# The first DFT step of a long convolution as 64-row by 64-column products, one channel half to a PSUM bank

## The chip, the cores and the metric

The kernel runs on one core of one Trainium2 chip, in one launch. The metric is the time of one execution on the device in microseconds (us). Engines are named as in the profile: PE is TensorE (PEld its weight loads), DVE is VectorE, ACT is ScalarE, POOL is GpSimd, SP is SyncE, which issues most of the DMAs.

## The reference

One block with two halves, on 2048 tokens and 640 channels, all in fp32: a gated long convolution, then an MLP over the tokens. The change lies in the convolution.

```python
def _A_ref(q, k, v, shift_k, ssm_k, ssm_D):
    # short causal convolution of k, 4 taps
    k_shift = sum of k_pad[:, t:t + S, :] * shift_k[:, ks - 1 - t]
    kv = k_shift * v
    # long causal convolution with ssm_k, per channel, over 2 S points
    y_f = rfft(kv padded to 2 S) * rfft(ssm_k padded to 2 S)
    y = irfft(y_f)[:S]
    y = y + kv * ssm_D
    return q * y

mod = (silu(c) @ w_mod)           # six rows: sa, ca, ga, sb, cb, gb
x = A_q
h = layernorm(x) * (1 + ca) + sa
x = x + ga * _A_ref(h, A_k, A_v, A_shift_k, A_ssm_k, A_ssm_D)
h = layernorm(x) * (1 + cb) + sb
x = x + gb * (W2 gelu(W1 layernorm(h)^T))^T
```

## The kernel before

**Tiling.** The 640 channels are worked in five chunks of 128 (`DC`, loop variable `c`). The 2048 tokens are split as n = 32 n1 + n2, with n1 on the 64 rows of a half of the partitions. The two halves of the 128 partitions hold the two halves of a chunk's channels (64 each), written `h` in the code; the 64 channels of a half are paired as index `i` (32 pairs) and `e` (2).

**The Fourier part of a chunk.** Each chunk has these stages, in this order on PE:

- `step1(0, t)`, t = 0 to 3: first DFT step of kv, over n1. The weights (stationary operand) are a column pick of `X`, 64 columns that stand 32 elements apart; the moving operand is `F1`, a constant matrix that holds cosines and sines. `F1` has 128 rows and, for each of cosine and sine (`ri`), 128 columns; it is block diagonal, since `_constants` fills only `f1[h, :, ri, h]`: the rows of channel half h meet the columns of channel half h, and the other two blocks are zero.
- `step1(1, t)`: the same for the convolution's kernel, with weights from `KSP`, whose 64 columns are contiguous. `perm` writes `KSP` into the tile `P`.
- `f2(g)`, g = 0 to 7: the second DFT step, over n2, with weights `W2` and the tile `z` as the moving operand; ACT copies the kernel's half into `kt`, DVE multiplies (`mul`), POOL adds (`add`) into `y`.
- `i2(r)` and `i1(half)`: the two steps of the inverse. Each `i2` ends in four copies (ACT, L282) into the upper half of tile `z`, which `i1` reads. `gate` multiplies the result into the output (DVE) and adds it to x (POOL).

The chunks overlap. While chunk c is in its inverse, the first step of chunk c + 1 is run between: in chunks 1 to 3 the order on PE is f2 (eight), step1(0, 0), step1(0, 1), i2(0), step1(0, 2), i2(1), step1(0, 3), i1(0), step1(1, 0), i1(1), step1(1, 1) to step1(1, 3), then f2 of the next chunk. Before the first chunk all eight calls of `step1` stand in a row, and chunk 0 has its own order, with the modulation's products between. The products of k's taps with v for later chunks (`kv_ops`, DVE, in chunk 0 also POOL) are laid into the gaps of DVE by hand: `dv(n)` issues the next n of the list `fill`. Every engine works through its instructions in the order written.

**One call of `step1`.** A call handles eight channel pairs i = 8 t + a. For each it issues two matmuls with the same weights, `ri` = 0 and 1, into partitions 0 to 63 and 64 to 127 of a PSUM tile of 1024 columns (two banks). Each takes 128 rows, 64 weight columns and 128 moving columns; a even goes to the first bank, a odd to the second. One ACT instruction (`evac`, L231) then copies the 1024 columns into `Z`, a view of tile `z` with the order side, t, a, k, e. For `step1(1, 0)` the copy is issued later (`later=True`), after the second gate.

**PSUM.** Three tiles of two banks go round (`ring`, `psum()`); a fourth, `tap`, is used for the taps. A product can start when the copy out of the tile three calls before is done.

After the five chunks comes the MLP (L443, L1051, L974), which the change does not touch.

Of the kernel before, what the change touches and what calls it, by code (L numbers as in the profile page):

```python
# [11 lines left out]
AF = mybir.ActivationFunctionType  # L12
# [38 lines left out]
def mixer_kernel(ctx: ExitStack, tc: tile.TileContext, q, k, v, shift_k, ssm_k, ssm_D, w1, b1, w2, b2, c,  # L51
# [7 lines left out]
    act, dve, pool, pe, sync = nc.scalar, nc.vector, nc.gpsimd, nc.tensor, nc.sync  # L59
# [3 lines left out]
    def mem(tag, n, name=None):  # L63

        return sb.tile([128, n], F32, name=name or tag, tag=tag, bufs=1)
# [4 lines left out]
    def psum(slot=None):  # L70

        uid[0] += 1
        slot = ring[uid[0] % len(ring)] if slot is None else slot
        return psp.tile([128, 1024], F32, name=f"pst_{uid[0]}", tag=f"pst{slot}", bufs=1)
# [6 lines left out]
    T_z, T_y, T_v1 = mem("z", 8192), mem("y", 4096), mem("v", 4520)  # L81
# [30 lines left out]
    F1, V2, ID, MK = SM[:, 0:256], SM[:, 256:384], SM[:, 384:420], SM[:, 420:422]  # L112
# [108 lines left out]
    def step1(side, t, later=False):  # L221

        ps = psum()
        for a in range(8):
            i = 8 * t + a
            lhs = KSP[:, i] if side else X.rearrange("p (m i) -> p i m", i=32)[:, i]
            o = 512 * (a % 2) + 128 * (a // 2)
            for ri in range(2):
                pe.matmul(ps[64 * ri:64 * ri + 64, o:o + 128], lhs, F1[:, 128 * ri:128 * ri + 128], start=True,  # L229
                          stop=True)  # L230
        evac = lambda: act.activation(Z[:, side, t].rearrange("p a k e -> p e a k"),  # L231
                                      ps.rearrange("p (e a k) -> p e a k", a=8, e=2), AF.Copy)
        return evac if later else evac()

    def f2(g):

        ps = psum()
        for kk in range(8):
            k1 = 8 * g + kk
            for ri in range(2):  # L240
                for h in range(2):
                    o = 128 * kk + 64 * ri
                    rhs = bass.AP(tensor=T_z.tensor, offset=T_z.offset + 128 * h + 2 * k1,
                                  ap=[T_z.ap[0], [256, 32], [1, 2]])
                    pe.matmul(ps[64 * h:64 * h + 64, o:o + 64], W2[k1 // 32][:, 2 * (k1 % 32) + ri], rhs, start=True, stop=True)  # L245
        pv = ps.rearrange("p (m s i) -> p m s i", s=2, i=32)
        xs_ = pv[:, :, 0]
        kt = KT[g % 2]
        act.activation(kt.rearrange("p (m i) -> p m i", i=32), pv[:, :, 1], AF.Copy)  # L249
        pa, pb = P[:, 1024 * (g % 2):1024 * (g % 2) + 512], P[:, 1024 * (g % 2) + 512:1024 * (g % 2) + 1024]  # L250
        m16 = lambda t: t.rearrange("p (m i) -> p m i", i=32)

        def mul():
            TT(dve, m16(pa), xs_, m16(kt), ALU.mult)
            sw = bass.AP(tensor=kt.tensor, offset=kt.offset + 32, ap=[kt.ap[0], [64, 8], [-32, 2], [1, 32]])
            TT(dve, pb.rearrange("p (k r i) -> p k r i", k=8, r=2), xs_.rearrange("p (k r) i -> p k r i", r=2), sw,
               ALU.mult)

        def add(eng=pool):
            for ri, t, op in ((0, pa, ALU.subtract), (1, pb, ALU.add)):  # L260
                t = t.rearrange("p (k r i) -> p r i k", k=8, r=2)
                TT(eng, Y[:, ri, :, 8 * g:8 * g + 8], t[:, 0], t[:, 1], op)
        return mul, add
# [20 lines left out]
    def i1(half, slot=None):  # L284

        ps = psum(slot)
        for jj in range(8):
            for ri in range(2):
                for e in range(2):
                    p = slice(64 * e, 64 * e + 64)  # L290
                    for b in range(2):
                        n2 = 16 * b + 8 * half + jj
                        pe.matmul(ps[64 * b:64 * b + 64, 512 * e + 64 * jj:512 * e + 64 * jj + 64],  # L293
                                  V1[p, ri, n2], T2[p, :, 32 * ri + n2], start=ri == 0, stop=ri == 1)
        return ps
# [200 lines left out]
    for t in range(4):  # L496
        step1(0, t)
        lay_w2(0, t)
# [3 lines left out]
    for t in range(4):  # L502
        step1(1, t)
# [19 lines left out]
    for c in range(NC):  # L523
# [3 lines left out]
        for g in range(8):  # L527
            m_, a_ = f2(g)
            if pend_m:
                pend_m()  # L530
            if pend_a:
                pend_a()
            pend_a, pend_m = (pend_m and pa_next), m_
            pa_next = a_
            if c:
                for f_ in ac[2 * g:2 * g + 2]:
                    f_()
            if cn is None and g < 4:

                act.activation(X[:, 512 * g:512 * g + 1], epsc, AF.Copy)  # L540
                for b in range(2):
                    sync.dma_start(X[64 * b:64 * b + 64, 512 * g:512 * g + 512],
                                   dram(w1, (16 * b + g) * F, [[32 * F, 64], [1, 512]]))
            if c == 0 and g < 4:
                lay_w2(1, g)
                if g == 3:
                    load_q()
            dv(-(-len(fill) // max(6 - g, 1)))
            if c and cn is not None and g == 3:
                perm_add(cn)  # L550
# [13 lines left out]
        if c == 0:  # L564
            mod_load(0, 4, P[:, 0:1920])
            for t in range(4):
                step1(0, t)
            ps = psum()
# [83 lines left out]
        for half in range(2):  # L652
            ps = i1(half)
# [37 lines left out]
    start = []  # L691
# [84 lines left out]
    ps = i1(1, s1)  # L776
# [122 lines left out]
    for f_ in range(4, NF):  # L899
        ps = psum().rearrange("p (h m) -> p h m", h=2)  # L900
# [128 lines left out]
    for s in range(NW):  # L1029
# [17 lines left out]
        for f_ in range(NF):  # L1047
            u = U[f_]
            for k, (w, r) in enumerate(((wh, 0), (wh, 2), (wl, 0))):
                for h in range(2):  # L1050
                    pe.matmul(acc[s][:, h, 0:320], w[:, f_].bitcast(F32R), u[r + h].bitcast(F32R),  # L1051
                              start=f_ == 0 and k == 0, stop=f_ == NF - 1 and k == 2)
# [61 lines left out]
```

## Time and profile before

| what | value |
| --- | --- |
| three runs | 705.26, 708.44, 709.94 us; median 708.44 us |
| profiled execution, first to last instruction | 705.8 us; no other time is given for it |
| mean granted TensorE clock | 0.985 |
| instructions in the profile | 20785 |
| PE / PEld busy | 644.5 / 624.2 us |
| DVE / ACT / POOL busy | 492.5 / 307.1 / 155.9 us |
| Fourier part | from the start to about 302 us |

How to read it: a row of the groups gives line, engine, operation, output<-inputs, shape and count, then busy time and the mean time of one in ns, then the engine's idle time before them and what ended it. A matmul's shape is "rows*weight columns, rows x moving columns". In the order of time the columns are start, length (us), engine, line and what, with the idle time before it in brackets. PE's records overlap, since several are in flight: the spacing of their starts, not the length of one, is what a product costs. "issue" is time in which the engine waited for nothing that the profile shows. Lines L60 and L443 are helpers and stand for many places.

### The profile page before, as it was taken

Reading aid. Unit: us, or ns where it says so; the run is one execution under the profiler, and the core shown is the slowest. Engines: PE = TensorE matmul, PEld = TensorE weight load, DVE = VectorE, ACT = ScalarE, POOL = GpSimd, SP = SyncE. Lnnn points to the kernel's source line nnn. Section 1 sums busy time; section 2 is a strip of 40 time slices with the busy share of each in tenths; the row PEclk is TensorE's granted clock in tenths of the full one; section 3 lists DMA queues with packets and bytes.
Section 4 is the critical chain, followed back from the end, with each engine's and each line's share of the span. In section 5 each row is a group of like instructions: output and inputs, shape, how many; then the busy total and the mean of one; then the engine's idle time right before and its main releaser. Section 6 shows DMA issues by size and latency. Waiting matters only on the chain.

```text
span 705.8 us, 20785 instructions
## 1 busy us (share of the span) xinstructions
PE 644.5 (91%) x9131; PEld 624.2 (88%) x9131; DVE 492.5 (70%) x861; ACT 307.1 (44%) x473; POOL 155.9 (22%) x135
## 2 busy tenths in 40 slices
PE   0699779989999989977899999999999999999997
PEld 0699469889999989777899999999999999999997
DVE  7778468969879638888884312311298979888886
ACT  0664554645745645556767223222334322333331
POOL 5297039615526428100010000000000000000000
PEclk9999979999999999999999999999999999999999
DMA  9968978446333522361303543354163243555511
GB/s 180 219 205 238 350 148 168 110 76 144 68 62 88 172 59 68 115 150 30 60 1 60 99 82 60 61 103 77 52 194 105 88 149 99 166 170 170 148 60 38
DMA packets 166672, 82.80 MB, mean 117 GB/s; under 512 B 89235, under 2 KB 157622, under 8 KB 166582
## 3 DMA queue, kind: packets, MB, share of 16 engines
q1 hardware_dynamic: 162034, 80.17, 46.0%
q10 hardware_dynamic: 4548, 1.31, 1.1%
q8 instruction: 71, 1.16, 0.7%
q14 instruction: 19, 0.16, 0.1%
HBM read 70.97 MB, written 10.49 MB: 115 GB/s over the span
## 4 chain that ended last, share of the span: by engine, by line
PE 65%; DVE 16%; ACT 4%; DMA 4%; POOL 4%; issue 3%; SPq 2%; ACTq 0%; DVEq 0%; POOLq 0%
PE pst L443 21%; PE pst L974 17%; PE pst L1051 7%; PE pst L229 7%; PE pst L245 6%; PE pst L274 4%; POOL y L60 3%; DVE tap L60 3%; PE pst L293 2%; DVE kt L60 2%; DVE p L60 2%; DMA aux<-in_w_mod_dram 2%; SPq L163 2%; DVE aux L60 1%; DVE y L60 1%
## 5 line engine op out<-in xcount | busy, mean ns | idle before, releaser
L245 PEld LDWEIGHTS pst<-z,w 128*64 128x64 f32 x2560 | 94.6, 141 | 7.9 <-ACT z L231 7.3
L245 PE MATMUL pst<-z,w 128*64 128x64 f32 x2560 | 95.8, 240 | 6.2 <-ACT z L231 6.1
L60 POOL TENSOR_TENSOR y<-p 128x256 f32<-128x256 f32 x72 | 92.3, 1341 | 22.4 <-DVE p L60 21.9
L60 DVE TENSOR_TENSOR p<-pst,kt 128x512 f32<-128x512 f32 x80 | 52.4, 691 | 23.8 <-ACT kt L249 15.5
L229 PE MATMUL pst<-v,x 128*64 128x128 f32 x640 | 44.3, 297 | 23.6 <-DVE x L60 23.6
L231 ACT ACTIVATE z<-pst 128x1024 f32<-128x1024 f32 x40 | 45.9, 1148 | 42.7 <-PE pst L229 23.1
L229 PEld LDWEIGHTS pst<-v,x 128*64 128x64 f32 x640 | 42.5, 220 | 24.1 <-POOL t L468 23.5
L847 ACT ACTIVATE pst<-pst,sm 128x640 f32<-128x640 f32 x14 | 10.7, 767 | 85.7 <-PE pst L443 85.7
L249 ACT ACTIVATE kt<-pst 128x512 f32<-128x512 f32 x40 | 25.1, 627 | 47.4 <-PE pst L245 26.6
L274 PEld LDWEIGHTS pst<-v,y 32*128 32x128 f32 x1280 | 38.1, 187 | 6.7 <-POOL y L60 3.8
L229 PE MATMUL pst<-v,p 128*64 128x128 f32 x640 | 39.6, 282 | 4.2 <-issue 2.2
L274 PE MATMUL pst<-v,y 32*128 32x64 f32 x1280 | 40.0, 272 | 3.8 <-DVE y L60 2.7
L974 PE MATMUL pst<-r_z,m_w 128*128 128x320 f32 x222 | 41.6, 309 | 0.7 <-DVE m_w L60 0.7
L229 PEld LDWEIGHTS pst<-v,p 128*64 128x64 f32 x640 | 36.9, 142 | 5.6 <-issue 2.9
L962 ACT ACTIVATE m_w<-m_v 128x896 fp32r<-128x896 f32 x24 | 22.2, 949 | 38.5 <-DVE m_v L60 23.1
L60 DVE TENSOR_TENSOR tap<-tap,kt 128x512 f32<-128x512 f32 x51 | 35.6, 698 | 1.3
L60 DVE TENSOR_TENSOR kt<-in,tap 128x512 f32<-128x512 f32 x51 | 35.0, 686 | 1.5
L974 PEld LDWEIGHTS pst<-r_z,m_w 128*128 128x128 f32 x222 | 34.8, 188 | 0.9 <-DVE m_w L60 0.9
L60 DVE TENSOR_TENSOR m_w<-m_v,m_w 128x896 fp32r<-128x896 f32 x24 | 26.0, 1088 | 9.5 <-ACT m_w L962 9.5
L282 ACT ACTIVATE z<-pst 128x512 f32<-128x512 f32 x38 | 21.5, 670 | 23.2 <-PE pst L274 23.2
L962 ACT ACTIVATE m_w<-m_p 128x896 fp32r<-128x896 f32 x12 | 11.5, 954 | 41.2 <-DVE m_p L60 24.4
L443 PE MATMUL pst<-r_z,wb0b 128*128 128x320 f32 x180 | 28.1, 310 | 0.9 <-DVE u_x L60 0.9
(278 smaller groups left out, 1436.9 us busy)
## 6 DMA issues: line engine op xcount, KB each, us to landing
x<-in_B_w_dram SPq DMA_DIRECT2D x22, 512.0 KB
m_v<-in_B_w_dram SPq DMA_DIRECT2D x15, 384.0 KB
x<-in_B_w_dram SPq DMA_DIRECT2D x14, 384.0 KB
aux<-in_A_ssm_k_dram SPq DMA_DIRECT2D x10, 512.0 KB
in<-in_A_k_dram SPq DMA_DIRECT2D x36, 128.0 KB
in<-in_A_v_dram SPq DMA_DIRECT2D x36, 128.0 KB
m_x<-xs SPq DMA_DIRECT2D x28, 160.0 KB
out_dram<-m_x SPq DMA_DIRECT2D x28, 160.0 KB
```

The lines of the kernel that those rows point to most:

```text
L60: TT = lambda eng, o, a, b, op: eng.tensor_tensor(o, a, b, op=op)
L163: sync.dma_start(KSR[64 * h:64 * h + 64].rearrange("p (i n) -> p i n", i=64), dram(ssm_k, (DC * c + 64 * h) * S, [[32, 64], [S, 64], [1, 3 ...
L229: pe.matmul(ps[64 * ri:64 * ri + 64, o:o + 128], lhs, F1[:, 128 * ri:128 * ri + 128], start=True, stop=True)
L231: evac = lambda: act.activation(Z[:, side, t].rearrange("p a k e -> p e a k"), ps.rearrange("p (e a k) -> p e a k", a=8, e=2), AF.Copy)
L245: pe.matmul(ps[64 * h:64 * h + 64, o:o + 64], W2[k1 // 32][:, 2 * (k1 % 32) + ri], rhs, start=True, stop=True)
L249: act.activation(kt.rearrange("p (m i) -> p m i", i=32), pv[:, :, 1], AF.Copy)
L274: pe.matmul(pp[qd // 2][:, o:o + 64], Y[p, ri, i:i + 2].rearrange("p i k -> p (i k)"), V2[p, 64 * ri:64 * ri + 64], start=ri == 0, stop=ri ...
L282: act.activation(o, i, AF.Copy)
L443: pe.matmul(ps[0:m, h, 0:320], w_.bitcast(F32R), r_[:, 320 * h:320 * h + 320].bitcast(F32R), start=first and i == 0, stop=last and i == 2)
L962: act.activation(W[n][0].bitcast(F32R), A[p, w_], AF.Copy)
L974: pe.matmul(bank[n], w[:, i].bitcast(F32R), r.bitcast(F32R), start=i == 0 and k == 0, stop=i == 6 and k == 2)
L1051: pe.matmul(acc[s][:, h, 0:320], w[:, f_].bitcast(F32R), u[r + h].bitcast(F32R), start=f_ == 0 and k == 0, stop=f_ == NF - 1 and k == 2)
```

## The change

Each matmul of `step1` becomes two, one for each channel half: rows 64 h to 64 h + 63 of the weights and of `F1`, and only the 64 columns of `F1` that are not zero for these rows. The outputs of half 0 go to the first bank of the PSUM tile, those of half 1 to the second. The order in PSUM is therefore (half, a, k), the copy reads it so, and the block order in `z` changes: the half is now the slowest index of a call's 1024 elements. `f2` reads its 64 moving elements accordingly, still as 32 runs of two, but in three levels in place of two.

```diff
         for a in range(8):
             i = 8 * t + a
             lhs = KSP[:, i] if side else X.rearrange("p (m i) -> p i m", i=32)[:, i]
-            o = 512 * (a % 2) + 128 * (a // 2)
             for ri in range(2):
-                pe.matmul(ps[64 * ri:64 * ri + 64, o:o + 128], lhs, F1[:, 128 * ri:128 * ri + 128], start=True,
-                          stop=True)
+                for h in range(2):
+                    r, o = slice(64 * h, 64 * h + 64), 512 * h + 64 * a
+                    pe.matmul(ps[64 * ri:64 * ri + 64, o:o + 64], lhs[r], F1[r, 128 * ri + 64 * h:128 * ri + 64 * h + 64],
+                              start=True, stop=True)
         evac = lambda: act.activation(Z[:, side, t].rearrange("p a k e -> p e a k"),
-                                      ps.rearrange("p (e a k) -> p e a k", a=8, e=2), AF.Copy)
+                                      ps.rearrange("p (a e k) -> p e a k", a=8, e=2), AF.Copy)
...
                     o = 128 * kk + 64 * ri
-                    rhs = bass.AP(tensor=T_z.tensor, offset=T_z.offset + 128 * h + 2 * k1,
-                                  ap=[T_z.ap[0], [256, 32], [1, 2]])
+                    rhs = bass.AP(tensor=T_z.tensor, offset=T_z.offset + 512 * h + 2 * k1,
+                                  ap=[T_z.ap[0], [1024, 8], [128, 4], [1, 2]])
```

## The prediction

> **What bounds the kernel now.** I read the page first, then the groups by shape, then TensorE's (PE's) order of time in the Fourier stage, where all edited lines run. The page:
>
> ```profile
> span 705.8 us, 20785 instructions
> PE 644.5 (91%) x9131; PEld 624.2 (88%) x9131; DVE 492.5 (70%) x861; ACT 307.1 (44%) x473; POOL 155.9 (22%) x135
> q8 instruction: 71, 1.16, 0.7%
> PE pst L443 21%; PE pst L974 17%; PE pst L1051 7%; PE pst L229 7%; PE pst L245 6%; PE pst L274 4%; POOL y L60 3%; DVE tap L60 3%; PE pst L293 2%; DVE kt L60 2%; DVE p L60 2%; DMA aux<-in_w_mod_dram 2%; SPq L163 2%; DVE aux L60 1%; DVE y L60 1%
> ```
>
> PE carries most of the chain, but the edited product, L229, has 7% of it, some 47 us. The third row is the one to remember: 1.16 MB of PE's program came in 71 packets, 16.3 KB each. PE ran 9131 products and 9131 weight loads, so an instruction is 1.16 MB / 18262 = 64 B, and a packet holds 256, that is 128 load-and-product pairs. An fp32 matmul makes two pairs (16 matmuls a call give 640 records of each kind per side over 20 calls).
>
> ```profile
> L245 PE MATMUL pst<-z,w 128*64 128x64 f32 x2560 | 95.8, 240 | 6.2 <-ACT z L231 6.1
> L60 POOL TENSOR_TENSOR y<-p 128x256 f32<-128x256 f32 x72 | 92.3, 1341 | 22.4 <-DVE p L60 21.9
> L229 PE MATMUL pst<-v,x 128*64 128x128 f32 x640 | 44.3, 297 | 23.6 <-DVE x L60 23.6
> L231 ACT ACTIVATE z<-pst 128x1024 f32<-128x1024 f32 x40 | 45.9, 1148 | 42.7 <-PE pst L229 23.1
> L229 PEld LDWEIGHTS pst<-v,x 128*64 128x64 f32 x640 | 42.5, 220 | 24.1 <-POOL t L468 23.5
> L229 PE MATMUL pst<-v,p 128*64 128x128 f32 x640 | 39.6, 282 | 4.2 <-issue 2.2
> L229 PEld LDWEIGHTS pst<-v,p 128*64 128x64 f32 x640 | 36.9, 142 | 5.6 <-issue 2.9
> ```
>
> The two sides of the first step differ: with X as weights, picked 32 elements apart, a load lasts 220 ns; with KSP, contiguous, 142 ns. Now chunk 1, where i1 (L293) and the KSP calls alternate:
>
> ```profile
> 148.03 2.10 PE L293 MATMUL pst<-z,v 64*64 64x64 f32 x128
> 150.06 0.66 PE L229 MATMUL pst<-v,p 128*64 128x128 f32 x8
> 151.70 1.53 PE L229 MATMUL pst<-v,p 128*64 128x128 f32 x24 [0.98 <-issue]
> 153.16 1.75 PE L293 MATMUL pst<-z,v 64*64 64x64 f32 x104
> 155.70 0.58 PE L293 MATMUL pst<-z,v 64*64 64x64 f32 x24 [0.80 <-issue]
> 156.21 5.46 PE L229 MATMUL pst<-v,p 128*64 128x128 f32 x96
> ```
>
> i1 already has the shape that the change makes: 64 rows, 64 columns, 64 moving, four tiles. Its spacing is (2.10 - 0.22) / 127 = 14.8 ns a pair. And PE stops twice in "issue", waiting for nothing the profile shows; between the two restarts stand 24 + 104 = 128 pairs, just one packet of program. I read both stops as PE out of instructions. The restarts are 4.00 us apart: where PE is quick, a packet of 128 pairs costs about 3.9 us (I take it a little under), 30 ns a pair.
>
> **The change part by part.** Each matmul becomes two with half the rows and half the moving columns. A call goes from 32 pairs to 64; over 40 calls that is 1280 pairs, 2560 instructions, 10 packets more. The evacuation still moves 1024 elements in one instruction. Its reads now run in 64s over two banks; the nearest row either way is its own 1148 ns, so zero, with ACT's idle time before it as cover; without that cover each 0.1 us more a call would be 4 us over the 40. f2's moving operand keeps its 32 runs of two, with other steps; zero is taken, its bounds are i1's 14.8 ns a pair (two tiles: 29.6) and 64 ns against its 95.8 / 2560 = 37.4.
>
> A KSP call now takes 1.75 us (54.5 ns x 32). Afterwards it takes 64 x 14.8 = 0.95 us while instructions last, and 64 x 30 = 1.95 us where they don't. An X call takes 2.05 us now, (2.28 - 0.30) / 31 = 64 ns a pair by the 197.04 row below, 10 ns over the KSP call with the same stream, so its loads limit it. The trace has no 64-row load with spread columns. Below, i1's 14.8 ns gives 0.95 us; above, 64 ns for each load whatever its rows gives 4.1 us. i1 shows loads to the two row halves overlapping, so I take half of 64 ns: 2.05 us, unchanged.
>
> [...]
>
> *First stage.*
>
> ```profile
> 23.57 9.43 PE L229 MATMUL pst<-v,x 128*64 128x128 f32 x128 [23.57 <-DVE x L60]
> 32.80 7.18 PE L229 MATMUL pst<-v,p 128*64 128x128 f32 x128
> 41.16 2.06 PE L245 MATMUL pst<-z,w 128*64 128x64 f32 x50 [1.17 <-ACT z L231]
> ```
>
> Eight calls bind PE for 16.4 us, then one evacuation, then f2. The X half stays. The KSP half needs two packets; if two are loaded at the start and the next is asked for when one is entered, the boundary falls by 33.0, the next at 36.9 to 38.5, and PE ends at 38.8 to 39.8, f2 starts at 40.0 to 40.9. I take -0.5 us. The four X calls at 60 to 68 us lead to a wait for weights and gain nothing:
>
> ```profile
> 77.27 1.28 PE L353 MATMUL tap<-aux,sm 128*32 128x320 f32 x12 [1.15 <-DMA aux<-in_w_mod_dram]
> ```
>
> *End of chunk 0.* The last two KSP calls wait for a bank that DVE reads:
>
> ```profile
> 104.00 5.38 PE L229 MATMUL pst<-v,p 128*64 128x128 f32 x64 [1.96 <-DVE aux L60]
> 110.58 1.62 PE L245 MATMUL pst<-z,w 128*64 128x64 f32 x38 [1.20 <-ACT z L231]
> ```
>
> They run at 84 ns a pair, slowed by 84 / 54.5. The packet arrives during that wait; 128 pairs at 14.8 ns slowed alike last 2.9 us, at half speed 3.8. Gain 1.6 to 2.4; I take -1.8 us.
>
> *Chunks 1 to 3.* Chunk 2 as the pattern, PE and two rows of ACT, then one piece of the chain:
>
> ```profile
> 187.37 3.58 PE L274 MATMUL pst<-v,y 32*128 32x64 f32 x120 [0.86 <-DVE y L60]
> 193.10 4.00 PE L274 MATMUL pst<-v,y 32*128 32x64 f32 x128
> 197.04 2.28 PE L229 MATMUL pst<-v,x 128*64 128x128 f32 x32
> 199.30 2.10 PE L293 MATMUL pst<-z,v 64*64 64x64 f32 x128
> 202.01 1.96 PE L229 MATMUL pst<-v,p 128*64 128x128 f32 x30 [0.25 <-issue]
> 203.90 2.53 PE L293 MATMUL pst<-z,v 64*64 64x64 f32 x128
> ```
> ```profile
> 190.97 2.30 ACT L282 ACTIVATE z<-pst 128x512 f32<-128x512 f32 x4 [1.57 <-PE pst L274]
> 196.97 2.28 ACT L282 ACTIVATE z<-pst 128x512 f32<-128x512 f32 x4 [2.62 <-PE pst L274]
> ```
> ```profile
> 206.49 1.22 DVE aux L60
> ```
>
> The X calls are covered on all sides: two stand before 187.37, where i2 waits for DVE anyway; one runs under ACT's copies up to 193.27, which give i2 its banks; one under those up to 199.25, which i1 reads. Quicker X calls buy nothing. What counts is the end of the second i1, 206.43, which releases DVE's gate and the chain behind it. By the X and KSP calls before it, the packet boundary near 202.01 moves by 28 x 64 instructions, exactly seven packets, so that stop stays. The next boundary comes 128 pairs later: now 30 pairs of the KSP call and 98 of i1, afterwards 62 and 66. It opens at 202.01 + 3.9 = 205.9, and 62 pairs remain: 206.8 + 0.2 = 207.0, +0.6 us. Chunk 1 likewise: boundary at 155.6, 56 pairs left, 156.7 against 156.28, +0.4 us. In chunk 3 f2 has no tap work beside it and PE itself is the chain:
>
> ```profile
> 251.99 0.33 PE L293 MATMUL pst<-z,v 64*64 64x64 f32 x4 [0.70 <-issue]
> 256.44 5.46 PE L229 MATMUL pst<-v,p 128*64 128x128 f32 x96
> 263.13 1.09 PE L245 MATMUL pst<-z,w 128*64 128x64 f32 x23 [1.23 <-ACT z L231]
> ```
>
> From 251.99 there come about 4 pairs of i1, 64 KSP, 128 i1 and 192 KSP, 388 in place of 260: packets open at 255.9, 259.8 and 263.7, a few pairs follow, then 1.1 us of evacuation: f2 at 265.1, +2.0 us.
>
> Sum: -0.5 - 1.8 + 0.4 + 0.6 + 2.0 = +0.7 us. The span becomes 706.5. The median of the runs shown, 708.44, is 2.6 us above that span, so the time is 709.1 us.
>
> **The rivals.** *Loads of spread columns do not overlap (slower).* Every X call then takes 4.1 us. First stage 4 x 2.05 = 8.2; the four at 60 us, half covered by the wait for weights, 4; in each of chunks 1 to 3 two calls cost 2.05 each and the two before i2 cost 4.1 less the 1.3 us that i2 waits now: 3 x 6.9 = 20.7. Together 33, less the 3 us of packet stops, which the longer calls hide: 738 us. It decides once a load costs over 32 ns. For it: 220 against 142 ns. Against: i1's loads.
>
> *Instructions are no limit (faster).* If those stops have another cause, the KSP calls keep 0.95 us: -0.8 in chunks 1 to 3 each (2.4), -1.6 more before f2 of chunk 4, where ACT's copies bind, -1.6 in the first stage (ACT's row of copies again), -1.8: 701 us. For it: the stops are not named by the profile. Against: their spacing of 128 pairs. [...]
>
> *f2 reads worse.* Each ns a pair is 0.5 us a chunk: 8 ns more give 4 us in chunks 0 and 4 and, past POOL's 16 x 1.34 = 21.5 us of work on y, about 2 in each other: 723 us. A better f2 gains almost nothing, as POOL is behind it.
>
> **How the numbers follow.** Forecast, 704 to 715: 0.60. Instructions no limit, around 701: 0.15. Loads serial, around 738: 0.12. f2 worse, around 723: 0.10. Other: 0.03. A measurement tells about 1% from no change, 7 us. Faster by that much takes most of the 701 case: 0.14. Slower takes the loads, most of f2, and a longer packet time of the forecast: 0.24. Same: 0.62. The range leaves out the serial loads and the far end of the 701 case: 699 to 725; the forecast's own is 704 to 715.
>
> **What would show it.** Right: 1280 L229 records of each kind a side in place of 640, KSP pairs at 15 ns between stops of 1 to 2 us, stops 128 pairs and about 3.9 us apart, X calls still 2 us, the second i1 ending half a microsecond later after i2's start, f2's 37 ns unchanged. Wrong: X calls of 4 us, no longer or more stops in "issue", f2 away from 37 ns, or a later stage that moves by more than the shift it is handed.

## The result and the profile after

The changed kernel takes 729.09 us (median of four runs, 726.61 to 731.03) beside 708.80 us for the kernel before (four runs, 705.26 to 709.94): a ratio of 1.028, 95% interval 1.024 to 1.032. The forecast was no change, 709.1 us with a range of 699 to 725. It was wrong by 20 us. The profiled execution took 728.95 us, with a span of 726.8 us (before: 705.8) and a mean granted TensorE clock of 0.946 (before: 0.985).

The page and the groups by shape, after. They answer to the first rows shown of before.

```profile
PE 645.9 (89%) x10411; PEld 625.6 (86%) x10411; DVE 493.3 (68%) x861; ACT 304.2 (42%) x473; POOL 156.8 (22%) x135
q8 instruction: 81, 1.33, 0.8%
```
```profile
L246 PE MATMUL pst<-z,w 128*64 128x64 f32 x2560 | 97.9, 244 | 7.2 <-ACT z L232 6.2
L232 ACT ACTIVATE z<-pst 128x1024 f32<-128x1024 f32 x40 | 44.1, 1122 | 54.3 <-PE pst L230 34.0
L230 PE MATMUL pst<-v,p 64*64 64x64 f32 x1280 | 27.3, 243 | 20.2 <-issue 14.0
```

PE's busy time hardly moves (644.5 to 645.9 us), the program has the ten packets more that were counted (71 to 81), and ACT's copy takes 1122 ns in place of 1148. What is new stands in the last row: 20.2 us of idle time ahead of the KSP records, 14.0 of them in "issue" (before: 4.2 and 2.2).

The windows by stage, before and then after. A row gives the stretch, its length, the busy time and records of PE, PEld, DVE, ACT and POOL, then the granted clock, the DMA share and GB/s. The stages are the first stage, f2 of chunk 0, the X calls and i2 after it, the rest of chunk 0, and the inverses of chunks 1, 2 and 3, each to the start of the next f2.

```profile
23.60:41.20 17.60, 16.43 (x258) 16.18 (x258) 12.60 (x19) 14.14 (x13) 6.56 (x6) 1.00 0.93 200
41.20:60.10 18.90, 18.90 (x514) 18.90 (x515) 13.16 (x21) 8.96 (x11) 18.70 (x15) 1.00 0.78 217
60.10:73.20 13.10, 12.46 (x261) 12.09 (x257) 11.78 (x35) 6.94 (x9) 5.48 (x5) 1.00 0.88 281
73.20:110.60 37.40, 27.77 (x588) 21.26 (x586) 23.02 (x41) 21.18 (x35) 11.98 (x9) 0.86 0.91 229
136.10:162.90 26.80, 23.76 (x696) 22.39 (x696) 20.67 (x25) 13.43 (x15) 4.76 (x2) 1.00 0.39 74
187.40:213.10 25.70, 24.09 (x698) 22.74 (x698) 20.70 (x25) 13.41 (x15) 4.77 (x2) 1.00 0.41 75
237.30:263.10 25.80, 23.90 (x696) 22.75 (x696) 12.99 (x36) 13.39 (x16) 4.77 (x2) 1.00 0.33 74
```
```profile
23.60:43.30 19.70, 12.97 (x512) 12.53 (x512) 13.13 (x19) 12.98 (x13) 9.99 (x8) 0.87 0.86 194
43.30:64.00 20.70, 20.69 (x516) 20.61 (x516) 12.84 (x20) 8.83 (x11) 15.50 (x13) 0.87 0.81 229
64.00:83.00 19.00, 16.14 (x389) 15.64 (x391) 16.79 (x50) 7.09 (x9) 5.32 (x5) 0.81 0.75 267
83.00:118.40 35.40, 24.78 (x712) 18.27 (x712) 16.75 (x22) 20.55 (x35) 12.78 (x10) 0.81 0.72 164
143.30:172.40 29.10, 22.68 (x890) 21.66 (x890) 21.96 (x27) 13.32 (x16) 4.74 (x2) 0.88 0.42 84
196.50:226.00 29.50, 26.15 (x888) 25.11 (x888) 20.04 (x24) 13.16 (x16) 4.74 (x2) 0.71 0.34 62
250.60:282.80 32.20, 24.46 (x897) 23.51 (x896) 13.20 (x37) 14.15 (x16) 4.74 (x2) 0.84 0.30 69
```

Row by row the stages change by +2.1, +1.8, +5.9, -2.0, +2.3, +3.8 and +6.4 us, 20.3 in all. Between them, the stretches of f2 and the first X calls of chunks 1 to 3 give back 0.6 (from the starts in the rows: 25.5, 24.5 and 24.2 us before, 24.9, 24.1 and 24.6 after). After the start of f2 of chunk 4 there are 444.0 us left in place of 442.7. That makes the 21.0 us of the span.

Now the column of the clock. Before, only one of these stages is under 1.00; after, all seven are. The clock records of the two traces hold two values, 1 and 0.5, so a mean of 0.71 over 29.5 us is 2 x 0.29 x 29.5 = 17 us at half clock. Added up in this way, the seven stages hold 66 us of half clock after and 10 before. In these records the stretches of half clock within the span last 3.4 or 6.8 us before, and 3.4, 6.8, 10.2 or 17.1 us after.

PE's order of time, after: the end of the first stage, the X calls and i2 behind f2 of chunk 0, the end of chunk 0, then chunks 1, 2 and 3.

```profile
34.18 2.09 PE L230 MATMUL pst<-v,p 64*64 64x64 f32 x128 [0.86 <-issue]
40.93 1.22 PE L230 MATMUL pst<-v,p 64*64 64x64 f32 x33 [4.65 <-issue]
...
73.27 1.44 PE L230 MATMUL pst<-v,x 64*64 64x64 f32 x37 [2.22 <-issue]
75.89 7.09 PE L275 MATMUL pst<-v,y 32*128 32x64 f32 x124 [0.64 <-ACT z L232]
...
113.72 3.49 PE L230 MATMUL pst<-v,p 64*64 64x64 f32 x128 [5.33 <-DVE aux L60]
...
158.79 1.04 PE L230 MATMUL pst<-v,p 64*64 64x64 f32 x56 [1.29 <-issue]
163.34 1.04 PE L294 MATMUL pst<-z,v 64*64 64x64 f32 x56 [2.46 <-issue]
167.62 3.48 PE L230 MATMUL pst<-v,p 64*64 64x64 f32 x120 [1.39 <-issue]
...
196.47 4.63 PE L275 MATMUL pst<-v,y 32*128 32x64 f32 x120 [0.46 <-DVE y L60]
201.03 2.31 PE L230 MATMUL pst<-v,x 64*64 64x64 f32 x64
203.26 7.28 PE L275 MATMUL pst<-v,y 32*128 32x64 f32 x128
212.68 3.50 PE L294 MATMUL pst<-z,v 64*64 64x64 f32 x128
...
260.51 4.11 PE L275 MATMUL pst<-v,y 32*128 32x64 f32 x68 [1.80 <-issue]
276.74 2.10 PE L230 MATMUL pst<-v,p 64*64 64x64 f32 x128 [1.81 <-issue]
281.29 0.33 PE L230 MATMUL pst<-v,p 64*64 64x64 f32 x4 [2.46 <-issue]
```

Two things are to be read here. First, the stops of a packet: PE restarts 128 pairs apart, 4.55 us apart in chunks 1 and 3 (158.79 to 163.34, 276.74 to 281.29), 4.28 at the next (167.62), and 6.75 in the first stage (34.18 to 40.93). That these stops are waits for program can be read in the trace's DMA records: in the changed kernel all 16 restarts behind a stop in "issue" in the Fourier part come 1.3 to 1.6 us after the end of a packet of queue q8. Second, the half clock: a call of i2 takes 7.28 us where it took 4.00, and i1 3.50 where it took 2.10, in a stretch of chunk 2 in which PE does not stop at all. The last idle time ahead of that stretch is 0.46 us (196.47), where before had 0.86 at full clock.

### The profile page after: what moved, and what is told of

Same layout as the page of the kernel before. It is cut to its first block, busy times and chain, and to the rows that moved or that the text cites. A ratio compares the mean times of both kernels' runs of the same rounds, so it can differ in the third digit from the quotient of the medians.

```text
span 726.8 us, 23346 instructions
## 1 busy us (share of the span) xinstructions
PE 645.9 (89%) x10411; PEld 625.6 (86%) x10411; DVE 493.3 (68%) x861; ACT 304.2 (42%) x473; POOL 156.8 (22%) x135
## 3 DMA queue, kind: packets, MB, share of 16 engines
q8 instruction: 81, 1.33, 0.8%
## 4 chain that ended last, share of the span: by engine, by line
PE 70%; DVE 12%; issue 5%; ACT 5%; POOL 4%; DMA 3%; ACTq 0%; SPq 0%; DVEq 0%
PE pst L444 21%; PE pst L975 17%; PE pst L246 9%; PE pst L230 8%; PE pst L1052 7%; PE pst L275 6%; POOL y L60 3%; PE pst L294 2%; DMA aux<-in_A_ssm_k_dram 2%; DVE tap L60 1%; DVE kt L60 1%; ACT z L232 1%; DVE aux L60 1%; PE tap L354 1%; DVE p L60 1%
## 5 line engine op out<-in xcount | busy, mean ns | idle before, releaser
L246 PE MATMUL pst<-z,w 128*64 128x64 f32 x2560 | 97.9, 244 | 7.2 <-ACT z L232 6.2
L246 PEld LDWEIGHTS pst<-z,w 128*64 128x64 f32 x2560 | 96.7, 146 | 8.4 <-ACT z L232 7.0
L60 POOL TENSOR_TENSOR y<-p 128x256 f32<-128x256 f32 x72 | 93.4, 1347 | 31.1 <-DVE p L60 30.7
L230 PE MATMUL pst<-v,x 64*64 64x64 f32 x1280 | 43.6, 297 | 26.6 <-DVE x L60 23.7
L232 ACT ACTIVATE z<-pst 128x1024 f32<-128x1024 f32 x40 | 44.1, 1122 | 54.3 <-PE pst L230 34.0
L230 PEld LDWEIGHTS pst<-v,x 64*64 64x64 f32 x1280 | 41.7, 218 | 27.7 <-issue 26.8
L275 PEld LDWEIGHTS pst<-v,y 32*128 32x128 f32 x1280 | 48.0, 226 | 6.6 <-issue 3.2
L275 PE MATMUL pst<-v,y 32*128 32x64 f32 x1280 | 50.2, 313 | 3.9 <-issue 1.8
L230 PE MATMUL pst<-v,p 64*64 64x64 f32 x1280 | 27.3, 243 | 20.2 <-issue 14.0
L230 PEld LDWEIGHTS pst<-v,p 64*64 64x64 f32 x1280 | 25.0, 157 | 21.9 <-issue 15.2
L294 PEld LDWEIGHTS pst<-z,v 64*64 64x64 f32 x1280 | 25.0, 160 | 8.0 <-issue 5.4
L294 PE MATMUL pst<-z,v 64*64 64x64 f32 x1280 | 26.6, 245 | 5.3 <-issue 4.3
```

What stands on the lines that cost most here:

```text
L60: TT = lambda eng, o, a, b, op: eng.tensor_tensor(o, a, b, op=op)
L230: pe.matmul(ps[64 * ri:64 * ri + 64, o:o + 64], lhs[r], F1[r, 128 * ri + 64 * h:128 * ri + 64 * h + 64], start=True, stop=True)
L275: pe.matmul(pp[qd // 2][:, o:o + 64], Y[p, ri, i:i + 2].rearrange("p i k -> p (i k)"), V2[p, 64 * ri:64 * ri + 64], start=ri == 0, stop=ri ...
```

## The experiments

Two theories stood after the result, both with the doubled instructions behind them. By the first, PE stops for its program, and the rest follows from the stops. By the second, the clock falls because the products are small, 64 by 64 where the largest of the page are 128 by 128, even where PE has no stop. A third held the new order in `z` and f2's three-level read to blame.

**The order alone.** The products stay as before, and write through a view of the bank that gives the new order; f2 reads as in the change.

```diff
-                pe.matmul(ps[64 * ri:64 * ri + 64, o:o + 128], lhs, F1[:, 128 * ri:128 * ri + 128], ...)
+                whole = ps.rearrange("p (e h b k) -> p e b h k", e=2, h=2, b=4)
+                pe.matmul(whole[64 * ri:64 * ri + 64, a % 2, a // 2], lhs, F1[:, 128 * ri:128 * ri + 128], ...)
```

> The matmuls of before (128 rows, 128 columns), but with the new block order in z and f2's new three-level read; the PSUM order is chosen so that the copy keeps its form. Theory A (PE's program arrives too slowly for twice the instructions, PE stops, and the clock falls after stops): same as before, 707 to 711 us, f2 at 37 ns a pair. Theory B (quarter products use the array too little, so the clock falls without stops): same, 707 to 711. Theory C (the new read order costs): over 712, f2 at 39 ns a pair or more at full clock.

Measured: 709.11 us beside 709.22, ratio 1.000 (0.997 to 1.004). f2's group is the one of before (95.8 us, 240 ns); the second row is an i2 of chunk 3:

```profile
L252 PE MATMUL pst<-z,w 128*64 128x64 f32 x2560 | 95.7, 240 | 6.2 <-ACT z L238 6.1
...
236.08 5.89 PE L281 MATMUL pst<-v,y 32*128 32x64 f32 x128 [0.80 <-DVE y L60]
```

So the third theory falls, and with it the rival "f2 reads worse". The 4 ns by which a record of L246 is longer in the changed kernel is then not the read's; f2 of chunk 0 ran there at a clock of 0.87. The second row matters below: i2 takes 5.89 us in place of 4, for the most part at half clock, though every product here has the shape of before.

**The KSP calls alone.** Only side 1 is quartered; the X calls stay whole.

```diff
+        split = side        # side 0: one product of 128 columns, written as in the first experiment
...
-                for h in range(2):
+                for h in range(2) if split else ():
```

> Only the KSP calls are split into quarters; the X calls keep 128 rows and 128 columns. 1280 more instructions on PE, 5 packets, half of what the change adds. Theory A: the stops of 1.5 to 5 us among the KSP calls remain and the half clock behind them in the first stage and in chunk 3 too; 716 to 724 us. Theory B: the X calls use the array as before, so the half-clock stretches over i2 go; 709 to 714 us, mean clock 0.97 or more.

Measured: 720.12 us, ratio 1.015 (1.009 to 1.021), clock 0.957 in the profiled run. Its order of time, in chunk 1 and over i2 of chunk 3:

```profile
158.18 1.04 PE L235 MATMUL pst<-v,p 64*64 64x64 f32 x56 [1.17 <-issue]
162.19 1.04 PE L300 MATMUL pst<-z,v 64*64 64x64 f32 x56 [1.91 <-issue]
...
247.66 6.16 PE L281 MATMUL pst<-v,y 32*128 32x64 f32 x120 [0.96 <-DVE y L60]
253.75 3.71 PE L231 MATMUL pst<-v,x 128*64 128x128 f32 x32
```

The stops are there, 4.0 us and 128 pairs apart in chunk 1. This edit speeds up the KSP calls and loses 11 us. What the second theory expected did not come: over four executions the clock is 0.957 to 0.969, and the half clock over i2 stays although the X calls are whole. i2 takes 6.16 us for 120 pairs, the X call behind it 3.71 us in place of 2.3, and by the clock records 24 us of the inverses of chunks 1 to 3 pass at half clock. With the i2 of the first experiment, this shows that the clock can fall over i2 without X calls in quarters.

**The X calls alone.** Only side 0 is quartered.

```diff
+        split = not side    # side 1: one product of 128 columns, written as in the first experiment
...
-                for h in range(2):
+                for h in range(2) if split else ():
```

> Only the X calls are split. 1280 more instructions, but at 2.05 us a call, 4.1 us a packet, where a packet takes 3.9 to 4.5. Theory A: few stops beyond those of before, mainly before the first wait for weights; 709 to 715 us, clock 0.97 to 0.985. Theory B: the clock halves over i2 behind the X calls; 715 to 722 us, clock 0.955 or less. Both: X pairs at 31 to 32 ns.

Measured: 716.79 us, ratio 1.010 (1.006 to 1.013). There is no stop for program ahead of i2 here, and yet:

```profile
128.00:168.00 40.00, 35.46 (x922) 33.73 (x921) 26.82 (x32) 17.60 (x21) 10.21 (x8) 0.79 0.40 83
```
```profile
134.05 5.94 PE L281 MATMUL pst<-v,y 32*128 32x64 f32 x128 [1.69 <-DVE y L60]
142.15 7.26 PE L281 MATMUL pst<-v,y 32*128 32x64 f32 x128
```

The clock is 0.79 over 40 us, and i2 takes 5.94 and 7.26 us. The only idle time of PE between 128 and 152 is the 1.69 us ahead of i2, of the kind that chunk 2 of before had (0.86) at full clock, and by the clock records the half clock lasts from 136.6 to 153.6, over 17 us of work without a gap. The inverses of chunks 1 to 3 hold 34 us of half clock, against 24 in the KSP-only kernel and none before. The time fits the second theory, the clock (0.963 to 0.983 over eight executions, median 0.967) lies between what the two expected. The two halves cost 1.5% and 1.0%, together most of the 2.8%.

**The same instruction count without quarter products.** The KSP calls are cut by columns only: two products of 64 columns, each with all 128 rows. The program grows as in the second experiment, the zero blocks are still multiplied.

```diff
-                pe.matmul(ps[64 * ri:64 * ri + 64, o:o + 128], lhs, F1[:, 128 * ri:128 * ri + 128], ...)
+                n = 64 if side else 128
+                for u in range(0, 128, n):
+                    pe.matmul(ps[64 * ri:64 * ri + 64, o + u:o + u + n], lhs, F1[:, 128 * ri + u:128 * ri + u + n], ...)
```

> Only the KSP calls change: each product is issued as two of 64 moving columns, still with all 128 rows, zero blocks included. As many instructions as with the KSP calls in quarters, but PE works as long as before or longer (64 pairs at 27 to 30 ns). Theory A: PE asks for a packet each 3.7 us in these calls, so the packets arrive late there too; the stages end nearly as late as with quarters, but PE idles less and the clock stays: 711 to 717 us. Theory B (the quarter form is at fault, not the count): 708 to 711 us.

Measured: 715.24 us, ratio 1.008 (1.004 to 1.011). Its order of time in chunk 1:

```profile
148.79 1.90 PE L231 MATMUL pst<-v,p 128*64 128x64 f32 x56 [0.99 <-issue]
153.07 1.04 PE L295 MATMUL pst<-z,v 64*64 64x64 f32 x56 [1.17 <-issue]
157.07 3.77 PE L231 MATMUL pst<-v,p 128*64 128x64 f32 x120 [0.66 <-issue]
```

This is the supply nearly by itself. The clock stays: 0.995 in the profiled execution, the fastest of the ten, and 0.979 to 0.990 in the others (the kernel before beside it: 0.969 to 0.993). The stops stand at the same records as in the changed kernel (56, 56 and 120 records follow them), 4.0 to 4.3 us apart, and the kernel loses 0.8%, 6 us. Not all of that need be stops: by the row 157.07 a pair takes (3.77 - 0.22) / 119 = 29.8 ns, so a call 1.91 us in place of 1.75, up to 3 us over the 20 calls. The stops are shorter than those of the second experiment (0.99, 1.17 and 0.66 us against 1.17, 1.91 and 1.25), with 29.8 ns a pair where KSP pairs in quarters ran at 14.7 in the changed kernel.

**Split only where it was reckoned to help.** By the prediction's own terms, six calls should gain: the first X call and two KSP calls of the first stage, the last two of chunk 0, and the last of all (n counts the calls of `step1`).

```diff
+        split = n in (0, 6, 7, 14, 15, 39)
```

> Six of the 40 calls in quarters, those that found a packet of program waiting: the first X call (PE at half clock), the last two KSP calls of the first stage, the last two of chunk 0, the last of chunk 3. Theory A (supply, and the clock falls behind stops and behind sparse stretches): no new stop over 1 us and no new half clock, -1.2 -1.3 -1.9 -0.9 = -5.3 us, 702 to 706 us, ratio 0.990 to 0.997. Rival (any quarter call costs, or waits for weights in chunk 0 take the first gains back): 707 us or more.

Measured: 711.00 us, ratio 1.001 (0.998 to 1.005). The expected gain did not come.

```profile
40.36 0.37 PE L238 MATMUL pst<-v,p 64*64 64x64 f32 x1 [2.60 <-issue]
```

The two KSP calls of the first stage are done but for one record by 40.36 - 2.60 = 37.76, and then wait for the packet with the last. The evacuation waits for that one record, so f2 starts at 41.91, later than before (41.16). The clock did not stay either: 0.963 to 0.982 over twelve executions (median 0.969), beside 0.976 to 0.990 (0.983) for the kernel before, and in the profiled one it is half for 6.8 us over i2 in each of chunks 2 and 3, where no product around i2 is changed.

**A dense product beside the X calls.** The X-only kernel again, with one added product ahead of each X call of chunks 1 to 3, with all rows, 128 columns and 256 moving columns of `F1`, into the bank that the call then overwrites.

```diff
+        if not side and n >= 16:
+            pe.matmul(ps[:, 0:256], F1[:, 0:128], F1, start=True, stop=True)
```

> X calls in quarters as in the X-only run (716.8 us); in chunks 1 to 3 each X call is led by one more matmul of 128 rows, 128 weight columns and 256 moving columns into its own PSUM tile, whose result is overwritten (4 instructions, some 0.45 us of full array each). Theory B (the clock falls because the array is too little used): the half-clock stretches over i2, 34 us in all in the X-only run, go or shrink under 10 us, clock 0.98 or more; each of 6 calls not covered by copies costs 0.5 us: 709 to 714 us. Rival (chance or the number of instructions sets the clock): half clock stays over 20 us and the time is 717 to 722.

Measured: 715.17 us, ratio 1.009 (1.006 to 1.011), a little over what was expected. The same stretch as in the X-only kernel:

```profile
128.00:168.00 40.00, 37.44 (x1097) 34.92 (x1094) 32.49 (x42) 20.03 (x27) 12.32 (x10) 1.00 0.49 102
```
```profile
138.30 0.70 PE L229 MATMUL pst<-v 128*128 128x256 f32 x2
141.14 3.80 PE L286 MATMUL pst<-v,y 32*128 32x64 f32 x128
```

With 0.70 us of dense work (the 0.45 expected was an estimate that no run shows) ahead of each sparse call of 2.3 us the clock is 1.00 in this stretch, and i2 takes 3.80 us again. It is no matter of one profile: over nine executions the clock is 0.974 to 0.990 (median 0.983), as in the kernel before, where the X-only kernel has a median of 0.967. The filler also covers the 1.69 us ahead of the first i2, so a part of that gap in the fall is not excluded; but in chunk 2 of the changed kernel the clock fell behind 0.46 us. As a remedy the filler is worth next to nothing (1.010 to 1.009): the 12 fillers are 12 x 0.70 = 8.4 us of added work, and how much of it is hidden was not measured.

**The filler in the changed kernel.** The same product ahead of the X calls from n = 8 on.

> The changed kernel with the same extra matmul ahead of each X call from chunk 0's inverse on (16 calls, 64 instructions). Theory A and B together: the half clock behind X calls (around 199 to 216 us in the changed kernel) goes, that behind the stops among KSP calls (first stage, end of chunks 1 and 3) stays; 722 to 728 us, clock 0.955 to 0.965. If stops alone set the clock: as the changed kernel or slower by the added work, 729 to 735 us.

Measured: 727.88 us, ratio 1.027 (1.022 to 1.031). Two windows, over the KSP calls of chunk 1 and the inverse of chunk 2:

```profile
160.00:175.00 15.00, 12.08 (x377) 11.56 (x378) 11.53 (x17) 5.81 (x7) 2.98 (x2) 0.66 0.77 163
195.00:222.00 27.00, 21.65 (x898) 20.16 (x894) 20.05 (x24) 13.13 (x15) 4.73 (x2) 1.00 0.36 67
```

The half clock over the X calls of chunk 2 is gone (0.71 to 1.00), the one over the KSP calls of chunk 1, with their stops, is not. So what is left there is not brought by the X calls; whether the stops bring it or the sparse KSP calls was not tried apart.

**Bulk loads against packets.** The changed kernel without the loads of k and v for chunk 1, some 2 MB.

```diff
     def kv_loads(c, g):
+        if c == 1:
+            return
```

> The changed kernel without the loads of k and v for chunk 1 (some 2 MB that are on their way during the first stage; chunk 1 then works on chunk 0's numbers, so its time is read for the first stage alone). Theory: a packet of program comes late where it waits behind bulk loads; the two restarts among the first stage's KSP calls, 6.75 us apart in the changed kernel, come 3.7 to 4.5 us apart, and f2 starts 2 us or more earlier after the first product. Rival (a packet takes what it takes, the long stop has another cause): 6 us or more apart as before.

Measured: one time, 723.70 us, beside 708.38 for the kernel before on the same chip. Its order of time, and below it that of the changed kernel with the filler, whose first stage is the changed kernel's with all its loads (the last row is its window):

```profile
33.27 2.43 PE L232 MATMUL pst<-v,p 64*64 64x64 f32 x128 [0.45 <-issue]
37.28 0.73 PE L232 MATMUL pst<-v,p 64*64 64x64 f32 x33 [1.57 <-issue]
```
```profile
34.85 2.09 PE L240 MATMUL pst<-v,p 64*64 64x64 f32 x128 [1.47 <-issue]
39.41 0.73 PE L240 MATMUL pst<-v,p 64*64 64x64 f32 x33 [2.47 <-issue]
```
```profile
23.60:41.30 17.70, 12.44 (x512) 12.06 (x512) 12.26 (x19) 14.53 (x13) 5.91 (x6) 1.00 0.94 221
```

Without the loads the two restarts stand 4.01 us apart in place of 6.75, and f2 starts at 39.18 in place of 43.31, as the theory had it. But the kernel with the filler has the loads in place, a DMA share of 0.94 over the stage (0.86 in the changed kernel), and its restarts are 4.56 us apart. So the loads alone do not make 6.75, and that the packet waited behind the transfers is not shown.

**Three calls.** What the run of six calls left of the reckoned gains: only the first X call and the last two KSP calls of chunk 0.

```diff
+        split = n in (0, 14, 15)
```

> Three calls in quarters: the very first X call (PE at half clock, 3.4 us now) and the last two KSP calls of chunk 0, which wait for a bank while their program is already there. If quarters help where program is at hand: -1.2 - 1.9 us, 705 to 707 us, ratio 0.993 to 0.999, the last two KSP calls in 3.5 us in place of 5.4. Rival (the gains are taken back by the wait for weights in chunk 0 and by more half clock): 708 to 711.

Measured: 709.35 us, ratio 1.002 (0.998 to 1.005).

```profile
104.66 3.69 PE L238 MATMUL pst<-v,p 64*64 64x64 f32 x128 [4.15 <-DVE aux L60]
109.56 2.72 PE L255 MATMUL pst<-z,w 128*64 128x64 f32 x46 [1.22 <-ACT z L241]
```

The local gain is there (3.69 us in place of 5.38, f2 at 109.56 in place of 110.58), but a measurement of this kernel does not show it. The gain reckoned for the first X call is not there even locally: the KSP calls start 9.09 us after the first product (23.34 to 32.43), before 9.23 (23.57 to 32.80). That call ran slowly before: its 32 pairs take 3.2 us (23.57 to 26.78), those of the next call 2.0. That this was half clock is not shown directly: the trace's clock records begin at 26.52, with full clock. No version tried is faster than the kernel before.

## Why the prediction was wrong, step by step

**Right.** The supply of PE's program was rightly read as a limit, and the packet as 128 pairs: the stops came 128 pairs apart and where they were reckoned (the second one of chunk 1 with the forecast 56 pairs of i1 left, row 163.34). KSP pairs run at (2.09 - 0.22) / 127 = 14.7 ns, forecast 14.8. An X call takes 2.31 us against 2.05 to 2.28, so loads of spread columns do overlap between the row halves. The copy is unmoved, and so is f2 at full clock. The last two KSP calls of chunk 0 went from 5.38 to 3.49 us: -1.9, forecast -1.8.

**The size of a packet's time.** This was the term of the sum that carried the chunks and the first stage: 3.9 us, "a little under" the 4.00 of one pair of restarts. Measured are 3.7 to 4.6 in chunks 1 to 3, and 6.75 in the first stage, which therefore came out at +2.1 in place of -0.5. In another execution of the same first stage (the changed kernel with the filler) it was 4.56, and f2 started 41.33 - 23.76 = 17.57 us after the first product, before 41.16 - 23.57 = 17.59: even there the gain did not come. The condition under which the sum placed the boundaries, two packets at hand at the start and the next asked for when one is entered, fits the changed kernel's first stage: counted back in 128 pairs from the restarts the boundaries lie at 26.63, 30.65 and 34.18, and the first three packets of q8 within the span begin to move at 27.50, 31.85 and 38.42. The third began 4.2 us after its boundary, the other two about 1. Why, and so why the one packet took 6.75 us, stays open: the DMA share does not explain it (0.86 there, 0.94 with 4.56). In chunk 3 the last restart came 281.29 - 250.60 = 30.7 us after the start of the stage, where the forecast had 263.7 - 237.3 = 26.4.

**X calls "unchanged".** Their duration was right, their need of program was overlooked. Before, a packet of X pairs lasted 128 x 64 ns = 8.2 us; now it lasts 128 x 31 ns = 3.9 us, which is the packet time itself. In the changed kernel the calls that stood at 60 to 68 us, counted at zero, met a stop of 2.22 us (restart at 73.27), and in chunk 3 one of 1.80 us cuts into i2 (260.51), in a place where before had none.

**The clock.** The sum had no term for it, and none of the rivals was about it: all stages were reckoned at the clock of before, without a reason given, and the changed kernel has 66 us of half clock in place of 10. Which of the misses is the larger the runs do not say. The X-only kernel shows that the half clock comes without long stops, the filler that it goes with denser work, the filler in the changed kernel that a part among the KSP calls remains. That X calls in quarters bring it is not shown: with whole X calls the clock fell over i2 as well (KSP alone, six calls, and once with the order alone), if for a shorter time in these profiles. What it costs in one place can be read in chunk 2, where a pair of i2 or i1 takes longer with no stop ahead of it: 7.28 - 4.00 for i2 and 3.50 - 2.10 for i1, 4.7 us; the stage as a whole became 3.8 longer, where the forecast had 0.6. In chunk 0 the i2 behind the X calls takes 7.09 in place of 3.79, which with the stop of 2.22 makes most of the +5.9.

**The rivals.** "Instructions are no limit" and "loads do not overlap" are out by the rows above, "f2 reads worse" by the first experiment. The list of what would show the forecast wrong did name "more stops in issue"; it held no line for the clock column.

**Idle time and the clock.** In two places a long wait stands at the half clock: the stop of 4.65 us in the first stage (half clock from 38.34 to 48.58, 0.87 over the f2 behind it), and the wait of 5.33 us at the end of chunk 0 (half clock from 113.43 to 116.85). The stops in "issue" of chunks 1 and 3 last 0.5 to 2.5 us, and the clock falls there too (from 164.63 to 171.46 and from 260.21 to 270.45). In the X-only kernel PE is busy for 35.46 of 40 us, and the clock is half for 17 us on end. So neither the length of a stop nor the share of busy time that a profile gives tells the clock here.

**What stays open.** What sets the clock: with denser work ahead of the sparse calls it was 1.00 over 40 us where it had been 0.79, but the runs do not say how dense the work has to be, nor why it falls over i2 in some kernels with whole X calls and not in others. How the 20 us divide between stops and clock: the column split, nearly supply alone, costs 0.8%, the X side alone 1.0%, and whether the two feed each other where KSP products are quick was not measured apart. Why the small gains of three and six split calls do not reach the total was not settled either; the clock is one candidate (median 0.976 and 0.969 over their executions, beside 0.986 and 0.983 for the kernel before).

## What to carry to other kernels

Before cutting a product into smaller ones, divide PE's instructions by the time that the stage will then have: where 128 load-and-product pairs would run in less than the 3.5 to 4.6 us that a packet took here (6.75 once), expect what was measured here: PE waited for its program, and nothing in the busy shares warned of it (PE 91% before, 89% after). Leaving out zeros also left PE with smaller products, and the clock fell (0.985 to 0.946), over the stages beside them too: read the clock column by stage, over several executions, and price a fall to half over neighbours such as i2 (4.00 to 7.28 us here). If the products on the path are bound by other things (here copies, gates and loads), what is saved on the array is worth nothing, and what is lost is not.

## What the runs showed of the hardware

- At half clock, not all work slows alike. i2 went from 4.00 to 7.28 us, while a quartered X call inside the same stretch kept its 2.31 us (201.03, between two slow calls). A whole X call did slow down, from 2.3 to 3.71 us (KSP alone, 253.75). Why the one keeps its time and the other does not was not tried apart.
- Where PE was out of program, packets of 16 KB let it restart 3.5 to 4.6 us apart, once 6.75 us. The transfer is the smaller part of it: by the page's row (0.8% of 16 engines' span of 726.8 us, for 81 packets) a packet takes about 1.1 us, PE restarts 1.3 to 1.6 us after its end, and in the traces of the kernel before and of the changed one no two packets of q8 start closer than 3.3 us (3.38 and 3.33). The rows agree on what a packet holds: 1.33 MB in 81 packets is 16.4 KB each, 1.33 MB over 2 x 10411 products and loads is 64 B an instruction, and the stops stand 128 pairs apart.
- A KSP product of half the rows and half the stream is 3.7 times as quick as the whole one (14.7 against 54.5 ns a pair) as long as instructions last.
